# The 64-row operands of the last sequence chunk given 128 rows, and the last chunk of q 128 columns

## The chip, the cores and the metric

The kernel runs on one core of a Trainium2 chip. A core has five engines that work side by side and meet at semaphores: TensorE (PE in the rows; PEld is its loading of the stationary operand), VectorE (DVE), ScalarE (ACT), GpSimd (POOL) and SyncE (SP), which here only issues transfers. The metric is the device time of one execution in microseconds, lower is better.

## The reference, cut to what matters

Three blocks follow each other over a batch of 8 sequences of 576 tokens. All is float32.

```python
kv  = einsum('bhsd,bhse->bhde', k, v)          # attention without softmax: k^T v, 8 heads of 64
out = einsum('bhsd,bhde->bhse', q, kv)
x   = out / sqrt(mean(out*out, -1) + 1e-6) * g_norm

u   = x + ((x^T @ U) @ V)^T                    # token mixing of rank 32, over the 576 tokens
x   = u + relu(u @ w_ch1) @ w_ch2              # 512 -> 2048 -> 512

h   = gelu(x @ w_in)                           # 512 -> 1024; u, v are its halves
v_n = layernorm(v) * g_ln
v_s = einsum('ts,bsd->btd', w_sg, v_n) + b_sg  # token mixing by a 576 x 576 matrix
out = x + (u * v_s) @ w_out
```

## The kernel before

The 576 tokens of a sequence are cut into five chunks of rows: c = 0 to 3 have 128 tokens, c = 4 has 64 (`rows(c)`). The stationary operand of a matmul has up to 128 rows (what is summed over) and 128 columns (the partitions of the result). A matmul on float32 data (`F32` tiles) runs as two instructions, one on data split beforehand into a high and a low part (`F32R` tiles) as one, so that three products stand for one product of full precision. A transpose is one instruction.

The program on TensorE stands in the order in which the Python code issues it; the other engines' instructions are ordered by a scheduler at build time, by priority, and each engine then runs its own in that order. SyncE issues all transfers in order.

The part up to about 290 us of the span does the attention, the low-rank mixing and six of the sixteen column blocks of w_ch1. It goes batch by batch after the list `PERIOD`, one period of about 35 us each, in which the work of three batches is mixed: `U` is `ch1` of batch b (24 matmuls of 288 columns), and for the next batch b+1 come `X0` to `X4` (`att_x`, one chunk of q times kv, then on ScalarE a square and a copy out of PSUM, and on VectorE a sum), `T0` to `T4` (`att_t`, x^T U) and `D0` to `D3` (`att_u`, which transposes x by 128 columns, adds the mixing and writes `u` in a high and a low part), and for batch b+2 `K0` to `K3` (`att_kv`, k^T v of one pair of heads). `D` ends a period; `X0` to `X3` begin the next one, and the first `U` after them reads what `D` wrote. In the first period (b = 0, list `FIRST`) and the last (b = 7) `U` follows `D` at once. In front of the first period stands a start without other work to mix with.

- `att_kv`: for each chunk the k columns of one head (64 columns) are stationary and v streams; two heads' results lie in the lower and the upper 64 partitions of `kvps`. Chunks 0 to 3 come from `kvm` with 128 rows, chunk 4 from `kvr` with 64.
- `att_x`: a chunk of q is stationary (128 rows, `n` columns: 128, or 64 for chunk 4).
- `att_u`: `PARTS` are tokens 0 to 255 and 256 to 575. In each part the chunks are transposed (x chunk stationary, the identity streams) into one PSUM tile, and one matmul adds the mixing. Chunk 4 has 64 rows.
- `unit_s`, in the last part of the program (from about 950 us): the mixing by w_sg. The stationary operand is a chunk of v_n (`vh`, `vl`), w_sg streams in two halves of 288 columns. Chunks 0 to 3 take three products; in chunk 4 high and low part of v lie above each other in one tile of 128 rows, with w_sg's 64 rows twice, so that the first product covers both; the second takes the 64 rows of the high part alone (`v[r]`). `r` is the lower or the upper half in turn.

The PSUM ring `ar` of four buffers serves `kvps`, `xps` and `ups`; `uso`, a ring of three, serves the last part.

Of the kernel before, what the change touches and what calls it, by code (L numbers as in the profile page):

```python
# [12 lines left out]
F32 = mybir.dt.float32  # L13
# [3 lines left out]
AF = mybir.ActivationFunctionType  # L17
ALU = mybir.AluOpType
AX = mybir.AxisListType
# [3 lines left out]
B, H, S, D = 8, 8, 576, 64  # L23
# [3 lines left out]
P = 128  # L27
NP = H // 2
NC = 5
# [14 lines left out]
def rows(c):  # L44
    return P if c < 4 else S - 4 * P
# [14 lines left out]
def tile_kernel(ctx: ExitStack, tc: tile.TileContext, kvm, kvr, qt, gcol, uv, w12,  # L60
# [5 lines left out]
    nc = tc.nc  # L66
    mm = nc.tensor.matmul
# [78 lines left out]
    pm = ph0.enter_context(tc.tile_pool(name="pm", bufs=1, space=PSUM))  # L146
    at = ExitStack()
    ap = at.enter_context(tc.tile_pool(name="ap", bufs=1, side="right"))
# [8 lines left out]
    ident = ap.tile([P, P], F32, tag="ident", name="ident")  # L157
# [3 lines left out]
    kvbd = ap.tile([P, NP, P], F32, tag="kvbd", name="kvbd")  # L161

    kv_t, q_t = {}, {}

    def load_kv(b, p):
        if b < 2 and p >= 2:
            x = spare[2 + b][:, (p - 2) * 5 * 2 * P:(p - 1) * 5 * 2 * P].rearrange("p (c k) -> p c k", c=5)
            m, r = x[:, :4], x[:S - 4 * P, 4]
        else:
            m = ap.tile([P, 4, 2 * P], F32, tag="kvm", bufs=2, name="kvm")  # L170
            r = ap.tile([S - 4 * P, 2 * P], F32, tag="kvr", bufs=2, name="kvr")
        nc.sync.dma_start(m, kvm[b, p])
        nc.sync.dma_start(r, kvr[b, p])
        kv_t[b, p] = (m, r)

    def load_q(b, p):
        q = ap.tile([P, S], F32, tag=f"q{p}", name=f"q{p}")
        nc.sync.dma_start(q, qt[b, p])
        q_t[b, p] = q

    w_raw, wh, wl = {}, {}, {}
    raws_at = [12, 13, 6, 7]
# [61 lines left out]
    at_s = {}  # L244
# [18 lines left out]

    def att_x(b, c):

        n = rows(c)
        if c == 0:
            at_s["ss", b] = small(b, "ss", 0)
            nc.gpsimd.memset(at_s["ss", b][64:, 4], 1.0)
        ps = pm.tile([P, H, D], F32, tag="ar", bufs=4, name="xps")  # L270
        for p in range(NP):
            mm(ps[:n, 2 * p:2 * p + 2, :], q_t[b, p][:, c * P:c * P + n], kvbd[:, p, :],  # L272
               start=True, stop=True)
        xn = xn_of(b, c)
        if b or c % 2 == 0:
            sq = ap.tile([P, H, D], F32, tag="sq", name="sq")
        else:
            sq = spare[4][:, 2700:2700 + DM].rearrange("p (h d) -> p h d", h=H)
        nc.scalar.activation(sq[:n], ps[:n], AF.Square)
        nc.scalar.activation(xn[:n], ps[:n], AF.Copy)  # L280
        nc.vector.tensor_reduce(at_s["ss", b][:n, c], sq[:n], AX.X, ALU.add)
        at_s["x", b, c] = xn

    def att_root(b):
# [7 lines left out]
    def att_norm(b, cs):  # L292

        y = at_s["y", b]
        for c in cs:
            n = rows(c)
            xn = at_s["x", b, c]
            nc.vector.tensor_tensor(xn[:n], xn[:n], y[:n, c].unsqueeze(2).to_broadcast([n, H, D]),
                                    ALU.mult)
            xf = xn.rearrange("p h d -> p (h d)")  # L300
            xh = ap.tile([P, DM], F32R, tag="xh", bufs=2, name="xh")
            xl = xh[n:] if c == 4 else ap.tile([P, DM], F32R, tag="xl", bufs=2, name="xl")
            nc.scalar.activation(xh[:n], xf[:n], AF.Copy)
            nc.vector.tensor_sub(xl[:n], xf[:n], xh[:n].bitcast(F32))
            at_s["x", b, c] = xf, xh, xl
# [18 lines left out]
    def att_u(b, d):  # L324


        if d == 0:
            us[b] = [up.tile([P, ND, S], F32R, tag="u32", bufs=2, name=n) for n in ("uh", "ul")]
        t4 = at_s["t4", b]
        ds = slice(d * P, (d + 1) * P)  # L330
        u = mp.tile([P, S], F32, tag="ut", bufs=3, name="ut")
        for o, e, cs in PARTS:
            ps = pm.tile([P, S - 256], F32, tag="ar", bufs=4, name="ups")[:, :e - o]
            for c in cs:
                n = rows(c)
                xf = at_s["x", b, c][0]
                mm(ps[:, c * P - o:c * P - o + n], xf[:n, ds], ident[:n, :n], is_transpose=True,
                   start=(c == cs[0]), stop=False)
            mm(ps, t4[:, ds], v4[:, o:e], start=False, stop=True)
            if o:  # L340
                nc.vector.tensor_scalar_mul(u[:, o:e], ps, g)
            else:
                nc.scalar.activation(u[:, o:e], ps, AF.Identity, scale=g)
        nc.sync.dma_start(ud[b][:, d], u)
        uh, ul = us[b]
        nc.scalar.activation(uh[:, d], u, AF.Copy)  # L346
        nc.vector.tensor_sub(ul[:, d], u, uh[:, d].bitcast(F32))  # L347
# [133 lines left out]
    for p in range(NP):  # L481
        load_q(0, p)
    nc.gpsimd.memset(kvbd, 0.0)
    make_identity(nc, ident)
    tmp_u = next_tmp()[:, :nu]
    in_turn(convert(uvr[0][:, :nu], tmp_u))
# [46 lines left out]
    for b in range(B):  # L533
        n, n2 = (i if i < B else None for i in (b + 1, b + 2))
        i = 0
# [4 lines left out]
        for s in PERIOD if b else FIRST:  # L540
            c = int(s[1:] or 0)
# [42 lines left out]
    pm = pha.enter_context(tc.tile_pool(name="pmb", bufs=1, space=PSUM, reuse_waits="tile"))  # L584
# [112 lines left out]
    while units:  # L697
        n = 3 if len(units) == 3 else 2
        two, units = units[:n], units[n:]
        a, b = two[0], two[-1]  # L700
# [16 lines left out]
        if b.j == len(BLOCKS) - 1 and b.i in (0, 1):  # L717
            y = up.tile([P, ND, S], F32, tag="u32", bufs=2, name="y0")
# [227 lines left out]
    def unit_s(n, f):  # L946
        if f == 0:
            gh[n] = up.tile([P, ND, S], F32R, tag="u32", bufs=2, name="gh")
            gl[n] = up.tile([P, ND, S], F32R, tag="u32", bufs=2, name="gl")
        ps = uso()  # L950
        s = slice(f * P, (f + 1) * P)
        for c in range(NC):
            wgh, wgl = p2["wsgh"][:, c], p2["wsgl"][:, c]
            if c < 4:
                terms = ((vh[c], wgh), (vh[c], wgl), (vl[c], wgh))
            else:
                r = slice(64 * (n % 2), 64 * (n % 2) + 64)
                v = (vh, vl)[n % 2][c]
                terms = ((v, wgh), (v[r], wgl[r]))
            for i, (a, w) in enumerate(terms):  # L960
                for e in range(2):
                    mm(ps[:, e, :HS], a[:, s], w[:, halves[e]], start=(c == 0 and i == 0),  # L962
                       stop=(c == NC - 1 and i == 1))
        o = g2u.pop((n, f))
        t = pb.tile([P, S], F32, tag="ut", bufs=2, name="sq")
        nc.vector.scalar_tensor_tensor(halved(t), ps[:, :, :HS], gl2[:, f:f + 1], halved(bs2),
                                       ALU.mult, ALU.add)
        nc.vector.tensor_mul(t, t, o)
        nc.scalar.activation(gh[n][:, f], t, AF.Copy)
        lo = nc.vector if n == B - 1 else nc.gpsimd  # L970
        lo.tensor_sub(gl[n][:, f], t, gh[n][:, f].bitcast(F32))
# [41 lines left out]
    for n in range(B):  # L1013
        p = n - 1
# [8 lines left out]
        for s in seq:  # L1023
            i = int(s[1])
# [29 lines left out]
    n = B - 1  # L1054
# [56 lines left out]
```

## Time and profile before

| | before |
|---|---|
| median of 3 runs (lowest to highest) | 1377.82 us (1377.21 to 1380.42) |
| span of the profiled execution | 1374.1 us |
| TensorE busy in it | 1341.0 us, 98% |
| VectorE, ScalarE, GpSimd busy | 56%, 39%, 21% |
| TensorE's part of the chain that ended last | 88% |
| instructions of TensorE | 8050 matmuls, 8050 loads |

The span is counted from the first to the last recorded instruction of one execution. That execution's own device time isn't listed apart; the span lies 3.7 us below the median of the runs, which holds what stands before the first and behind the last instruction. A busy TensorE isn't a TensorE at its peak: a matmul's record is longer than the step from its start to the next one's start, because they overlap. So the text below works with starts.

### The profile page before, as it was taken

How to read it: one execution, taken by the hardware profiler on the slowest of the kernel's cores; microseconds unless marked ns; L12 is line 12 of the kernel's file. 1: busy time of each engine (PE TensorE's matmuls, PEld its weight loads, DVE VectorE, ACT ScalarE, POOL GpSimd, SP SyncE). 2: the span in 40 equal slices, each digit the busy share in tenths (PEclk: the TensorE clock that was granted, in tenths of full speed). 3: DMA queues.
4: the chain of work that ended last, by engine and by line, in shares of the span. 5: the costliest groups of instructions: out<-in, count | busy, mean ns of one | idle time of the engine just before them, and what ended most of it. 6: DMA issues, size and time to landing. Idle time of an engine off the chain costs nothing.

```text
span 1374.1 us, 20734 instructions
## 1 busy us (share of the span) xinstructions
PE 1341.0 (98%) x8050; PEld 1174.8 (85%) x8050; DVE 771.7 (56%) x1405; ACT 535.4 (39%) x888; POOL 284.7 (21%) x268
## 2 busy tenths in 40 slices
PE   6799999999999999999999999999999999999998
PEld 5599999997877789888888888889899999999998
DVE  4767777755765742322232234547676675775874
ACT  4665666654544532311211213445333333323321
POOL 0411001101111000200000001245253452543332
PEclk9999999999999999999999999999999999999999
DMA  9556665355766776835543545531021120110001
GB/s 347 191 190 221 218 214 182 107 180 185 271 221 220 245 261 244 318 93 170 167 144 114 171 161 192 168 108 44 1 70 36 35 70 18 52 53 18 36 18 52
DMA packets 86930, 199.44 MB, mean 145 GB/s; under 512 B 12208, under 2 KB 33456, under 8 KB 85040
## 3 DMA queue, kind: packets, MB, share of 16 engines
q1 hardware_dynamic: 86832, 198.12, 43.2%
q8 instruction: 63, 1.03, 0.3%
q14 instruction: 35, 0.29, 0.1%
HBM read 126.00 MB, written 72.09 MB: 144 GB/s over the span
## 4 chain that ended last, share of the span: by engine, by line
PE 88%; DVE 4%; ACT 1%; DMA 1%; issue 0%; POOL 0%; SPq 0%; DVEq 0%; ACTq 0%
PE acc L350 10%; PE acc L351 10%; PE acc L352 9%; PE uso L962 9%; PE uso L983 7%; PE uso L874 6%; PE c L350 4%; PE c L352 3%; PE c L351 3%; PE y L350 3%; PE y L352 3%; PE y L351 3%; PE v L350 2%; PE v L351 2%; PE v L352 2%; PE xps L272 2%
## 5 line engine op out<-in xcount | busy, mean ns | idle before, releaser
L350 PE MATMUL acc<-yx,w 128*128 128x512 f32 x576 | 224.1, 389 | 0.0
L352 PE MATMUL acc<-yx,w 128*128 128x512 f32 x576 | 224.1, 389 | 0.0
L351 PE MATMUL acc<-yx,w 128*128 128x512 f32 x576 | 224.1, 389 | 0.0
L772 DVE SCALAR_TENSOR_TENSOR yx<-yr,yx 128x1024 fp32r<-128x1024 f32 x70 | 85.8, 1226 | 244.1 <-ACT yx L771 237.1
L771 ACT ACTIVATE yx<-yr 128x1024 fp32r<-128x1024 f32 x70 | 74.3, 1061 | 277.4 <-PE acc L352 264.4
L350 PEld LDWEIGHTS acc<-yx,w 128*128 128x128 f32 x576 | 108.1, 188 | 22.6 <-ACT y L604 0.2
L352 PEld LDWEIGHTS acc<-yx,w 128*128 128x128 f32 x576 | 108.1, 188 | 22.5
L351 PEld LDWEIGHTS acc<-yx,w 128*128 128x128 f32 x576 | 108.1, 188 | 22.2
L350 PE MATMUL c<-uh,w 128*128 128x288 f32 x384 | 116.7, 304 | 0.7 <-ACT uh L346 0.7
L351 PE MATMUL c<-ul,w 128*128 128x288 f32 x384 | 113.6, 296 | 1.8 <-DVE ul L347 1.8
L352 PE MATMUL c<-uh,w 128*128 128x288 f32 x384 | 113.4, 295 | 0.8 <-POOL w L126 0.6
L874 PE MATMUL uso<-zh,wio 128*128 128x288 f32 x512 | 94.2, 298 | 0.6 <-DVE g2u L882 0.4
L983 PE MATMUL uso<-gh,wio 128*128 128x288 f32 x512 | 93.1, 296 | 0.0
L109 POOL TENSOR_TENSOR tmp<-tmp,wior 128x512 int32<-128x512 int32 x12 | 15.7, 1309 | 314.7 <-DVE tmp L108 269.8
L983 PEld LDWEIGHTS uso<-gh,wio 128*128 128x128 f32 x512 | 77.9, 188 | 2.3 <-issue 0.2
L350 PE MATMUL y<-T,c 128*128 128x512 f32 (+1 forms) x200 | 75.3, 376 | 4.1 <-DVE y L602 3.7
L874 PEld LDWEIGHTS uso<-zh,wio 128*128 128x128 f32 x512 | 76.3, 188 | 3.2 <-issue 1.3
L350 PEld LDWEIGHTS c<-uh,w 128*128 128x128 f32 x384 | 72.0, 188 | 4.1 <-issue 1.0
L351 PEld LDWEIGHTS c<-ul,w 128*128 128x128 f32 x384 | 72.1, 188 | 3.8 <-DVE ul L347 2.9
L351 PE MATMUL y<-T,c 128*128 128x512 f32 (+1 forms) x200 | 74.5, 372 | 0.0
L352 PE MATMUL y<-T,c 128*128 128x512 f32 (+1 forms) x200 | 74.5, 372 | 0.0
L352 PEld LDWEIGHTS c<-uh,w 128*128 128x128 f32 x384 | 72.1, 188 | 1.3 <-POOL w L126 0.9
(210 smaller groups left out, 2916.4 us busy)
## 6 DMA issues: line engine op xcount, KB each, us to landing
yr<-yd SPq DMA_DIRECT2D x70, 512.0 KB, 3.7
yd<-y SPq DMA_DIRECT2D x92, 256.0 KB, 3.4
kvm<-kvm_dram SPq DMA_DIRECT2D x28, 512.0 KB, 4.6
raw<-w_dram SPq DMA_DIRECT2D x26, 512.0 KB, 4.2
q<-qt_dram SPq DMA_DIRECT2D x32, 288.0 KB, 4.8
ud<-ut SPq DMA_DIRECT2D x32, 288.0 KB, 2.1
z<-ud SPq DMA_DIRECT2D x8, 1152.0 KB, 6.4
out_dram<-ot SPq DMA_DIRECT2D x31, 288.0 KB, 2.1
```

What stands on the lines that cost most here:

```text
L109: yield behind(nc.gpsimd.tensor_add(t, t, low))
L272: mm(ps[:n, 2 * p:2 * p + 2, :], q_t[b, p][:, c * P:c * P + n], kvbd[:, p, :], start=True, stop=True)
L350: mm(ps, ah, bh, start=start, stop=False, **kw)
L351: mm(ps, ah, bl, start=False, stop=False, **kw)
L352: mm(ps, al, bh, start=False, stop=stop, **kw)
L771: nc.scalar.activation(yh, y, AF.Relu)
L772: nc.vector.scalar_tensor_tensor(yl, y, 0.0, yh.bitcast(F32), ALU.max, ALU.subtract)
L874: mm(ps[:, e, :HS], a[:, s], c[:, halves[e]], start=(d == 0 and i == 0), stop=(d == ND - 1 and i == 2))
L962: mm(ps[:, e, :HS], a[:, s], w[:, halves[e]], start=(c == 0 and i == 0), stop=(c == NC - 1 and i == 1))
L983: mm(ops[d][:, e, :HS], a[:, s], c[:, f, halves[e]], start=(f == 0 and i == 0), stop=(f == ND - 1 and i == 2))
```

## The change

Each operand of 64 rows becomes one of 128 rows, with zeros or with a second copy in the added rows.

- `kvr` and the spare tiles that hold its data in the first two batches have 128 rows; the lower half is set to zero by GpSimd (two tiles at the start for all batches, one memset for each of the four spare slices). The transfers write the upper half, as before.
- q lives in four fixed tiles `q_of` of 640 columns; the last 64 are set to zero once, in four memsets. Chunk 4 of `att_x` takes 128 columns, so that its results have 128 rows, the lower 64 of them zero. The eight memsets on `ss` that kept the unused rows harmless are gone.
- `att_u` transposes chunk 4 with 128 rows and 128 columns; the PSUM tile has 384 columns instead of 320, of which 320 are used.
- `unit_s` takes the whole `v` and `wgl` in the second product of chunk 4: the low part times the low part is added to the sum.

```diff
@@ -162,21 +162,28 @@
 
     kv_t, q_t = {}, {}
 
+    rest = [ap.tile([P, 2 * P], F32, tag=f"kvr{i}", name="kvr") for i in range(2)]
+    q_of = [ap.tile([P, NC * P], F32, tag=f"q{p}", name=f"q{p}") for p in range(NP)]
+    for r in rest:
+        nc.gpsimd.memset(r[rows(4):], 0.0)
     def load_kv(b, p):
         if b < 2 and p >= 2:
             x = spare[2 + b][:, (p - 2) * 5 * 2 * P:(p - 1) * 5 * 2 * P].rearrange("p (c k) -> p c k", c=5)
-            m, r = x[:, :4], x[:S - 4 * P, 4]
+            m, r = x[:, :4], x[:, 4]
+            nc.gpsimd.memset(r[rows(4):], 0.0)
         else:
             m = ap.tile([P, 4, 2 * P], F32, tag="kvm", bufs=2, name="kvm")
-            r = ap.tile([S - 4 * P, 2 * P], F32, tag="kvr", bufs=2, name="kvr")
+            r = rest[p % 2]
         nc.sync.dma_start(m, kvm[b, p])
-        nc.sync.dma_start(r, kvr[b, p])
+        nc.sync.dma_start(r[:rows(4)], kvr[b, p])
         kv_t[b, p] = (m, r)
 
     def load_q(b, p):
-        q = ap.tile([P, S], F32, tag=f"q{p}", name=f"q{p}")
-        nc.sync.dma_start(q, qt[b, p])
-        q_t[b, p] = q
+        nc.sync.dma_start(q_of[p][:, :S], qt[b, p])
+        q_t[b, p] = q_of[p]
 
     w_raw, wh, wl = {}, {}, {}
     raws_at = [12, 13, 6, 7]
@@ -263,22 +270,20 @@
 
     def att_x(b, c):
 
-        n = rows(c)
         if c == 0:
             at_s["ss", b] = small(b, "ss", 0)
-            nc.gpsimd.memset(at_s["ss", b][64:, 4], 1.0)
         ps = pm.tile([P, H, D], F32, tag="ar", bufs=4, name="xps")
         for p in range(NP):
-            mm(ps[:n, 2 * p:2 * p + 2, :], q_t[b, p][:, c * P:c * P + n], kvbd[:, p, :],
+            mm(ps[:, 2 * p:2 * p + 2, :], q_t[b, p][:, c * P:(c + 1) * P], kvbd[:, p, :],
                start=True, stop=True)
         xn = xn_of(b, c)
         if b or c % 2 == 0:
             sq = ap.tile([P, H, D], F32, tag="sq", name="sq")
         else:
             sq = spare[4][:, 2700:2700 + DM].rearrange("p (h d) -> p h d", h=H)
-        nc.scalar.activation(sq[:n], ps[:n], AF.Square)
-        nc.scalar.activation(xn[:n], ps[:n], AF.Copy)
-        nc.vector.tensor_reduce(at_s["ss", b][:n, c], sq[:n], AX.X, ALU.add)
+        nc.scalar.activation(sq, ps, AF.Square)
+        nc.scalar.activation(xn, ps, AF.Copy)
+        nc.vector.tensor_reduce(at_s["ss", b][:, c], sq, AX.X, ALU.add)
         at_s["x", b, c] = xn
 
     def att_root(b):
@@ -295,8 +300,7 @@
         for c in cs:
             n = rows(c)
             xn = at_s["x", b, c]
-            nc.vector.tensor_tensor(xn[:n], xn[:n], y[:n, c].unsqueeze(2).to_broadcast([n, H, D]),
-                                    ALU.mult)
+            nc.vector.tensor_tensor(xn, xn, y[:, c].unsqueeze(2).to_broadcast([P, H, D]), ALU.mult)
             xf = xn.rearrange("p h d -> p (h d)")
             xh = ap.tile([P, DM], F32R, tag="xh", bufs=2, name="xh")
             xl = xh[n:] if c == 4 else ap.tile([P, DM], F32R, tag="xl", bufs=2, name="xl")
@@ -330,11 +334,11 @@
         ds = slice(d * P, (d + 1) * P)
         u = mp.tile([P, S], F32, tag="ut", bufs=3, name="ut")
         for o, e, cs in PARTS:
-            ps = pm.tile([P, S - 256], F32, tag="ar", bufs=4, name="ups")[:, :e - o]
+            full = pm.tile([P, NC * P - 256], F32, tag="ar", bufs=4, name="ups")
+            ps = full[:, :e - o]
             for c in cs:
-                n = rows(c)
                 xf = at_s["x", b, c][0]
-                mm(ps[:, c * P - o:c * P - o + n], xf[:n, ds], ident[:n, :n], is_transpose=True,
+                mm(full[:, c * P - o:(c + 1) * P - o], xf[:, ds], ident, is_transpose=True,
                    start=(c == cs[0]), stop=False)
             mm(ps, t4[:, ds], v4[:, o:e], start=False, stop=True)
             if o:
@@ -481,6 +485,8 @@
     for p in range(NP):
         load_q(0, p)
     nc.gpsimd.memset(kvbd, 0.0)
+    for q in q_of:
+        nc.gpsimd.memset(q[:, S:], 0.0)
     make_identity(nc, ident)
     tmp_u = next_tmp()[:, :nu]
     in_turn(convert(uvr[0][:, :nu], tmp_u))
@@ -954,9 +960,8 @@
             if c < 4:
                 terms = ((vh[c], wgh), (vh[c], wgl), (vl[c], wgh))
             else:
-                r = slice(64 * (n % 2), 64 * (n % 2) + 64)
                 v = (vh, vl)[n % 2][c]
-                terms = ((v, wgh), (v[r], wgl[r]))
+                terms = ((v, wgh), (v, wgl))
             for i, (a, w) in enumerate(terms):
                 for e in range(2):
                     mm(ps[:, e, :HS], a[:, s], w[:, halves[e]], start=(c == 0 and i == 0),
```

The order on TensorE is the same but for the shapes. The next rows are TensorE's, in `D0` to `D1` of batch 1 (end of the first period), of before and then of the change; `ups` is the PSUM tile, `xn` the normalized chunk, `t` the mixing's operand, and the sizes are those of what is written.

```order
L337 MATMUL ups<-ident,xn 128x128 x2
L339 MATMUL ups<-v_119,t_836 128x256
L337 MATMUL ups<-ident,xn 128x128 x2
L337 MATMUL ups<-ident,xn 128x64
L339 MATMUL ups<-v_119,t_836 128x320
L337 MATMUL ups<-ident,xn 128x128 x2
```

```order
L341 MATMUL ups<-ident,xn 128x128 x2
L343 MATMUL ups<-v_119,t_828 128x256
L341 MATMUL ups<-ident,xn 128x128 x3
L343 MATMUL ups<-v_119,t_828 128x320
L341 MATMUL ups<-ident,xn 128x128 x2
```

The transpose of chunk 4 writes 128 columns instead of 64; nothing stands at another place.

GpSimd's first work after its constants, before and then with the change; `kvbd` is the block-diagonal kv, `ident` the identity.

```order
L483 MEMSET kvbd 128x512
masks.py:197 MEMSET ident 128x128
L269 MEMSET spare_127 64x8
L269 MEMSET ss 64x8
masks.py:199 ISA
masks.py:199 AFFINE_SELECT ident<-ident 128x128
L109 TENSOR_TENSOR tmp_121<-tmp_121,uv_140 128x160
```

```order
L170 MEMSET kvr 64x256 x2
L176 MEMSET spare_133 64x256 x2
L487 MEMSET kvbd 128x512
L489 MEMSET q_123 128x64
L489 MEMSET q_124 128x64
L489 MEMSET q_125 128x64
L489 MEMSET q_126 128x64
masks.py:197 MEMSET ident 128x128
L176 MEMSET spare_134 64x256
masks.py:199 ISA
masks.py:199 AFFINE_SELECT ident<-ident 128x128
L176 MEMSET spare_134 64x256
```

Ten memsets of zeros stand among the first, two small ones are gone, and `kvbd` comes fifth.

VectorE's work around the first `D0` to `D3` (batch 0, end of the start), before and then with the change; `ny` and `nt` are the reciprocal root of batch 1, `ut` and `ul` belong to `D`, `xn` and `xl` to the chunks of batch 1.

```order
L341 TENSOR_SCALAR ut<-ups,g 128x320
L94 SCALAR_TENSOR_TENSOR ny<-nt,ny 128x40
L92 TENSOR_TENSOR nt<-ny 128x40
L93 SCALAR_TENSOR_TENSOR nt<-nt,ss 128x40
L94 SCALAR_TENSOR_TENSOR ny<-nt,ny 128x40
L347 TENSOR_TENSOR ul<-ut,uh 128x576
L341 TENSOR_SCALAR ut<-ups,g 128x320 x2
L298 TENSOR_TENSOR xn<-xn,ny 128x512
L347 TENSOR_TENSOR ul<-ut,uh 128x576 x2
L341 TENSOR_SCALAR ut<-ups,g 128x320
L304 TENSOR_TENSOR xl<-xn,xh 128x512
L298 TENSOR_TENSOR xn<-xn,ny 128x512
```

```order
L345 TENSOR_SCALAR ut<-ups,g 128x320
L92 TENSOR_TENSOR nt<-ny 128x40
L93 SCALAR_TENSOR_TENSOR nt<-nt,ss 128x40
L94 SCALAR_TENSOR_TENSOR ny<-nt,ny 128x40
L303 TENSOR_TENSOR xn<-xn,ny 128x512
L351 TENSOR_TENSOR ul<-ut,uh 128x576
L345 TENSOR_SCALAR ut<-ups,g 128x320 x2
L308 TENSOR_TENSOR xl<-xn,xh 128x512
L351 TENSOR_TENSOR ul<-ut,uh 128x576 x2
L345 TENSOR_SCALAR ut<-ups,g 128x320
L303 TENSOR_TENSOR xn<-xn,ny 128x512 x2
L351 TENSOR_TENSOR ul<-ut,uh 128x576
```

One scaling of a chunk (`xn`) more stands ahead of the fourth `ul`, and the first `ut` one small instruction later. From the second period on VectorE's order differs in sizes alone but for one exchange in the first period, and ScalarE's by an exchange of neighbours in `X0` and `X1`.

## Rows read from the trace of the kernel before

**Rows 1.** The page, first part: busy time, share of the span, instructions.

```profile
PE 1341.0 (98%) x8050; PEld 1174.8 (85%) x8050; DVE 771.7 (56%) x1405; ACT 535.4 (39%) x888; POOL 284.7 (21%) x268
```

**Rows 2.** Busy time by stretch; behind the engines: granted clock, share of DMA, GB/s.

```profile
114.71:123.17 8.46, 8.18 (x63) 7.05 (x61) 5.48 (x9) 6.54 (x13) 0.00 (x0) 1.00 0.58 212
540.00:920.00 380.00, 380.00 (x1678) 314.77 (x1677) 126.95 (x167) 98.15 (x112) 33.09 (x26) 1.00 0.52 173
950.00:1365.00 415.00, 413.41 (x2721) 384.77 (x2720) 282.66 (x605) 136.43 (x217) 166.15 (x159) 1.00 0.11 35
```

**Rows 3.** Whom TensorE waited for: us in total, times, longest.

```profile
PE ups L339 <- DVE nt L92: 7.3, 1, 7.3
...
PE c L351 <- DVE ul L347: 1.8, 4, 0.7
PE tp L315 <- DVE xl L304: 1.4, 2, 1.1
```

**Rows 4.** Timeline of TensorE, chunk 4 of one unit_s (start, length, rows*columns, count).

```profile
1304.43 0.43 PE L962 MATMUL uso<-wsgh,vh 128*128 128x288 f32 x2
1304.79 0.52 PE L962 MATMUL uso<-wsgl,vh 64*128 64x288 f32 x2
1305.24 0.53 PE L962 MATMUL uso<-wsgh,vh 128*128 128x288 f32 x2
1305.61 0.42 PE L962 MATMUL uso<-wsgl,vh 128*128 128x288 f32 x2
1305.87 0.43 PE L962 MATMUL uso<-wsgh,vl 128*128 128x288 f32 x2
```

**Rows 5.** Timeline of TensorE, end of one att_kv, from narrow windows (last instructions of each).

```profile
112.53 0.29 PE L255 MATMUL kvps<-kvm 128*64 128x64 f32 x4
...
112.59 0.23 PE L255 MATMUL kvps<-kvm 128*64 128x64 f32 x2
112.75 0.27 PE L255 MATMUL kvps<-kvr 64*64 64x64 f32 x2
...
112.85 0.23 PE L255 MATMUL kvps<-kvr 64*64 64x64 f32 x2
113.01 0.40 PE L350 MATMUL c<-uh,w 128*128 128x288 f32 x1
```

**Rows 6.** Timeline of TensorE, D0 of batch 2 and the start of D1.

```profile
114.71 0.38 PE L337 MATMUL ups<-ident,xn 128*128 128x128 f32 x2
...
115.05 0.58 PE L337 MATMUL ups<-ident,xn 128*128 128x128 f32 x3
...
115.81 0.38 PE L337 MATMUL ups<-ident,xn 128*128 128x128 f32 x2
```

**Rows 7.** Timeline of TensorE, X0 and X1 (two windows), then X4 of batch 3.

```profile
119.13 1.05 PE L272 MATMUL xps<-kvbd,q 128*128 128x128 f32 x8
...
119.13 1.95 PE L272 MATMUL xps<-kvbd,q 128*128 128x128 f32 x16
...
124.70 0.29 PE L352 MATMUL c<-uh,w 128*128 128x288 f32 x1
124.92 1.09 PE L272 MATMUL xps<-kvbd,q 128*64 128x128 f32 x8
...
126.18 0.30 PE L351 MATMUL c<-ul,w 128*128 128x288 f32 x1
```

**Rows 8.** Timeline of ScalarE, the square of X0 of batch 3; in brackets the idle time before.

```profile
120.22 0.60 ACT L279 ACTIVATE sq<-xps 128x512 f32<-128x512 f32 x1 [0.65 <-PE xps L272]
```

**Rows 9.** Timeline of TensorE, waits in the first and in the last period.

```profile
66.94 0.40 PE L352 MATMUL c<-uh,w 128*128 128x288 f32 x1 [0.63 <-POOL w L126]
...
293.59 0.40 PE L351 MATMUL c<-ul,w 128*128 128x288 f32 x1 [0.23 <-DVE ul L347]
```

**Rows 10.** Timeline of the start: the first memset, and the first chunk of 64 rows.

```profile
0.74 0.53 POOL L483 MEMSET kvbd<- 128x512 f32 x1 [0.29 <-POOLq L1096]
...
5.30 0.37 PE L255 MATMUL kvps<-kvr 64*64 64x64 f32 x2
```

## The prediction

> **What bounds the kernel now.** First the page's list of busy engines: TensorE is busy for 98% of the span [rows 1]. That alone doesn't say that it sets the pace everywhere, so the busy time by stretch comes next: from 540 to 920 us it has no gap, in the last part (950 to 1365 us) 1.6 us of 415, and around a `D` to `X` passage (114.71 to 123.17 us) 0.3 us of 8.5 [rows 2]. The list of waits agrees: single waits at the start and around `D` and `T`, nearly none later [rows 3]. So a step that TensorE saves comes off the span, unless the next thing it needs isn't ready. What it could save is read from the starts in its timeline, since the records overlap.
>
> **What an operand of 64 rows costs.** In `unit_s`, with 128 rows, two matmuls of 288 columns take 0.26 us from start to start (1305.61 to 1305.87) [rows 4]. Around chunk 4 the pairs start at 1304.43, 1304.79, 1305.24 and 1305.61: 1.18 us for three pairs, where 3 x 0.26 = 0.78 would do [rows 4]. The 0.40 us aren't work, since the 64-row pair streams the same 288 columns. They come half on the way into 64 rows and half on the way out, and TensorE names no releaser for them. I read them as the price of going from one array shape to another and back, about 0.2 us each way. By the Trainium skill (TensorEngine Tiling (Array Packing), Key Properties) a change of tiling mode drains TensorE; the rows agree, and as it gives no figure the sum is made from the rows.
>
> **The change, part by part.**
>
> `unit_s`: 32 visits (8 batches of 4 units), each with its two shape changes gone and nothing added, since the second product streams 288 columns either way: 32 x 0.39 = 12.5 us (0.39 and not 0.40, as the starts have two decimals). The stretch has 1.6 us of waits in all and VectorE is busy for 283 of 415 us, so I take all of it as span [rows 2].
>
> `att_u`: a `D` takes 115.81 - 114.71 = 1.10 us; its first part, two transposes of 128 and a matmul of 256 columns, takes 0.34 [rows 6]. The second part will be three transposes and 320 columns without a change of shape; scaled by streamed columns, 0.34 x 704 / 512 = 0.47. So a `D` takes 0.81 and saves 0.29, four save 1.16. What is late next? ScalarE and VectorE empty the PSUM tiles. In the `D` to `X` passage ScalarE is busy 6.54 us of 8.46 [rows 2], and in front of the square of `X0` it sat idle for 0.65 us until TensorE had finished `X0` [rows 8]. With a passage of 7.3 us it still fits, with little left; I count 1.1 instead of 1.16 in the six periods where `X` follows `D` (batches 1 to 6): 6.6 us. After the `D` of batch 7 the next `U` waits for VectorE's `ul` already [rows 9]; there I count 0.4 of 1.16, since the first `ut` comes earlier by only a part. The `D` of batch 0 lies in the start, see below: 0.
>
> `att_x`, chunk 4: from the last matmul before it (124.70) to the second after it (126.18) 1.48 us [rows 7]. With 128 columns throughout: eight instructions take 1.95 - 1.05 = 0.90 us (`X1` alone), plus 0.13 for each of the two `U` matmuls that belong to the stretch: 1.16, so 0.31 saved [rows 4, 7]. The added columns of the load cost next to nothing: the 64-column chunk has a record of 1.09 us, `X0` with 128 columns one of 1.05 [rows 7]. In five of the eight batches it lies in a period whose next wait is far enough away: 5 x 0.31 = 1.6 us. In batch 7's `T` TensorE waits for VectorE's `xl`, whose chain starts at the squares [rows 3]: there the 0.31 are lost and about 0.3 us more of the saved time turns into waiting, -0.3.
>
> By the Trainium skill (TensorE: Matmul & The Clock Gate, LDWEIGHTS) a load's time goes with its columns, not its rows: 64 more columns would add an estimated 53 ns to each of 64 loads, 3.4 us, were they not hidden. The rows speak against that, as the loads lie beside matmuls. For the added rows the same rule says no cost, as I assume.
>
> `att_kv`: pairs of 128-row instructions start 0.06 apart (112.53, 112.59), the pair of `kvr` comes after 0.16, the next after 0.10, and the `U` matmul 0.16 later: 0.42 from the last `kvm` pair [rows 5]. With 128 rows the operand has the shape of `kvm`: 0.06 + 0.06 + 0.16 = 0.28. The change of shape at the end stays, since 64 columns remain. 0.14 saved; 24 visits in the periods, of which the first two stand ahead of a wait in the first period (below): 22 x 0.14 = 3.1 us.
>
> The start and the first period: ten memsets of 64 rows come first on GpSimd. `kvbd` with 512 columns took 0.53 us [rows 10]; at that rate the four ahead of it take 4 x 0.27 = 1.1 us, and all ten no more than 2.6. The first matmul of 64 rows starts at 5.30 us [rows 10], so they lie under the first transfers; no transfer waits for them in SyncE's order. Uncovered they'd cost up to 2.6 us once. Later the start hangs on VectorE: TensorE waits 7.3 us in it [rows 3], so the 64-row visits before that are worth nothing there, but for an estimated 0.3 us (the last `kvr` of batch 0 and its `X4`, some 0.15 each) ahead of VectorE's first work. The new order puts one more scaling of 512 columns ahead of the fourth `ul` of batch 0; a square of 512 columns takes ScalarE 0.60 [rows 8], and about 0.6 I take for this. TensorE then waits at 66.94 for weights that GpSimd and VectorE split behind it [rows 9]. So nothing from ahead of 67 us comes through, and 0.3 us net are lost.
>
> **The sum.** 12.5 + 6.6 + 0.4 + 1.6 - 0.3 + 3.1 - 0.3 = 23.6 us. The span goes from 1374.1 to 1350.5. The median of the runs shown lies 3.7 us above the span; I take the same distance: 1377.8 - 23.6 = 1354.2 us.
>
> **Rivals.**
>
> *All of it arrives*: every visit at its full price, 32 x 0.39 + 32 x 0.29 + 8 x 0.31 + 32 x 0.14 = 12.5 + 9.3 + 2.5 + 4.5 = 28.8 us, 1349.0. For it: the six passages show little waiting. Against: waits stand behind the first and the last `D` [rows 3, 9].
>
> *The first part swallows its share*: ScalarE and VectorE set the pace of `D`, `X` and `T`, and of 11 us there half or all is waited for again. That gives 1360 to 1365. For it: 6.54 us of ScalarE's work in a passage that shrinks to 7.3 [rows 2]. Against: its 0.65 us of idle time, which would have to vanish first [rows 8].
>
> *The change of rows isn't what costs*: the 0.4 us come from chunk 4's operands themselves (the upper half of a tile, a stop of the group), and remain. Then only the start's 0.3 us and some 0.01 us an `X4` are added: 1378. Against: `att_kv`, `att_u` and `att_x` show delays of like size in other operands with nothing in common but the shape [rows 5 to 7].
>
> *Slower, through the clock*: a fuller array makes TensorE's granted clock fall in the last part. A stretch of t us that falls from the upper level (2.4 GHz) to the lower (1.2) takes t longer; to eat the 23.6 us, 23.6 of the 415 us would have to run at the lower one (a mean grant of 0.94), and at 0.90 the time would be 1396. Against: from 540 to 920 us all operands have 128 rows and no gap, and the grant is 1.00 [rows 2].
>
> **How the numbers follow.** Forecast 0.68 (19 to 27 us, 1351 to 1359), all of it 0.12, swallowed 0.14, no effect 0.04, slower 0.02. A difference of 0.3% (4.1 us) is about what a measurement of this kernel can tell from none. The first three are faster: 0.94; same 0.04; slower 0.02. The predicted time is 1354.2. The range takes in the forecast, the full price and the nearer third of the swallowed case: 1349 to 1361; left out are some 0.15.
>
> **What would show it.** In the changed profile: pairs of `unit_s` at 0.26 us throughout, no record with 64 rows on TensorE, 64 columns left in `att_kv` alone; the stretch between the first and the last `unit_s` shorter by some 12 us; a `D` of 0.81 us; each period of the first part shorter by 4 x 0.29 + 0.31 + 4 x 0.14 = 2.0 us. Wrong would be: gaps of 0.2 us that remain around chunk 4; waits of TensorE for `xn` or `ul` of 1 us in each period; a grant below 1.00 behind 950 us.

## The result and the profile after

| | before | after |
|---|---|---|
| median, 4 runs each (lowest to highest) | 1378.59 us (1377.21 to 1380.42) | 1354.05 us (1352.97 to 1354.84) |
| ratio, 95% interval | | 0.9824 [0.9812, 0.9836] |
| span of the profiled execution | 1374.1 us | 1352.0 us |

The time fell by 24.5 us; 23.6 were forecast, and the predicted 1354.2 us lies 0.15 us from the measured median.

The first line of the page, which answers to [rows 1], shows that TensorE is still busy nearly throughout. Its part of the chain that ended last is 83% of the span (88% before), VectorE's 8% (4% before). Its busy time fell by 26.1 us, 4.0 more than the span. VectorE, ScalarE and GpSimd have what they had, to 2 us.

```profile
PE 1314.9 (97%) x8050; PEld 1170.9 (87%) x8050; DVE 773.5 (57%) x1405; ACT 533.4 (39%) x888; POOL 286.0 (21%) x270
```

The next rows answer to [rows 2]: busy time by stretch of the kernel after, columns as there. Both stretches begin and end with the same instructions of TensorE as before, to within one matmul.

```profile
112.64:119.94 7.30, 7.02 (x62) 6.83 (x61) 5.56 (x10) 6.25 (x13) 0.00 (x0) 1.00 0.71 261
938.81:1343.02 404.21, 401.79 (x2721) 383.09 (x2720) 282.61 (x605) 135.99 (x217) 166.00 (x159) 1.00 0.11 36
```

The `D` to `X` passage is 1.16 us shorter (8.46 to 7.30), four times 0.29. The last part is 10.8 us shorter (415.00 to 404.21), and in it TensorE idles 2.4 us where it idled 1.6. The granted clock is 1.00 in both: a fuller array hasn't lowered it.

The list of TensorE's waits after (us in total, times, longest) answers to [rows 3].

```profile
PE ups L343 <- DVE nt L92: 7.5, 1, 7.5
...
PE c L355 <- DVE ul L351: 2.5, 5, 0.7
...
PE tp L319 <- DVE xl L308: 1.7, 2, 1.1
PE uso L880 <- DVE g2u L888: 1.4, 3, 0.6
PE uso L967 <- DVE g2u L888: 0.9, 1, 0.9
PE acc L355 <- DVE yx L778: 0.8, 1, 0.8
```

The big wait of the start is the same. Those for `ul` (1.8 before), `xl` (1.4) and for VectorE's `g2u` in the last part (0.4 and 0.9) have grown by 0.7, 0.3 and 1.0 us. So VectorE takes back about 2 us in all: it was on time for the old pace and is a little late for the new one. The wait for `yx` is a new row, of which more below.

The visits themselves, from TensorE's timeline after: chunk 4 of a `unit_s` for [rows 4], then the same view of an `att_kv` for [rows 5], `D0` of batch 2 for [rows 6] and an `X4` for [rows 7].

```profile
1284.99 0.43 PE L967 MATMUL uso<-wsgh,vh 128*128 128x288 f32 x2
1285.26 0.42 PE L967 MATMUL uso<-wsgl,vh 128*128 128x288 f32 x2
1285.52 0.43 PE L967 MATMUL uso<-wsgh,vh 128*128 128x288 f32 x2
1285.79 0.42 PE L967 MATMUL uso<-wsgl,vh 128*128 128x288 f32 x2
```

```profile
109.97 0.30 PE L356 MATMUL c<-uh,w 128*128 128x288 f32 x1
110.20 0.69 PE L262 MATMUL kvps<-kvm 128*64 128x64 f32 x16
110.71 0.29 PE L262 MATMUL kvps<-kvr 128*64 128x64 f32 x4
110.93 0.40 PE L354 MATMUL c<-uh,w 128*128 128x288 f32 x1
111.17 0.30 PE L355 MATMUL c<-ul,w 128*128 128x288 f32 x1
...
112.64 0.38 PE L341 MATMUL ups<-ident,xn 128*128 128x128 f32 x2
112.77 0.37 PE L343 MATMUL ups<-v,t 128*128 128x256 f32 x1
112.98 0.49 PE L341 MATMUL ups<-ident,xn 128*128 128x128 f32 x3
113.22 0.40 PE L343 MATMUL ups<-v,t 128*128 128x320 f32 x1
113.45 0.38 PE L341 MATMUL ups<-ident,xn 128*128 128x128 f32 x2
...
121.47 0.30 PE L356 MATMUL c<-uh,w 128*128 128x288 f32 x1
121.61 1.05 PE L277 MATMUL xps<-kvbd,q 128*128 128x128 f32 x8
122.42 0.38 PE L354 MATMUL c<-uh,w 128*128 128x288 f32 x1
122.63 0.29 PE L355 MATMUL c<-ul,w 128*128 128x288 f32 x1
```

In `unit_s` the pairs start 0.26 to 0.27 us apart throughout, where the steps around chunk 4 were 0.36, 0.45 and 0.37 [rows 4]. A `D` takes 113.45 - 112.64 = 0.81 us. Around `X4` it is 122.63 - 121.47 = 1.16. No operand has 64 rows any more; 64 columns remain in `att_kv` alone, and there 0.22 us still pass from the start of the `kvr` record (four instructions) to the next `U` matmul.

ScalarE's square of `X0` of batch 3 after, for [rows 8]:

```profile
117.00 0.60 ACT L284 ACTIVATE sq<-xps 128x512 f32<-128x512 f32 x1
```

The 0.65 us for which it sat idle ahead of this square are gone: ScalarE now comes from work of `D` straight to it. Its reserve in the passage is used up, but it isn't late: the square starts 1.09 us behind the first matmul of its `X0`, as before (119.13 to 120.22, [rows 7, 8], and 115.91 to 117.00).

### The profile page after: what moved, and what is told of

Read it like the earlier page. It is cut to its first block, busy times and chain, and to the rows that moved or that the text cites. A ratio compares the mean times of both kernels' runs of the same rounds, so it can differ in the third digit from the quotient of the medians.

```text
span 1352.0 us, 20734 instructions
## 1 busy us (share of the span) xinstructions
PE 1314.9 (97%) x8050; PEld 1170.9 (87%) x8050; DVE 773.5 (57%) x1405; ACT 533.4 (39%) x888; POOL 286.0 (21%) x270
## 3 DMA queue, kind: packets, MB, share of 16 engines
q8 instruction: 63, 1.03, 0.3%
## 4 chain that ended last, share of the span: by engine, by line
PE 83%; DVE 8%; DMA 4%; ACT 3%; issue 2%; POOL 0%; SPq 0%; DVEq 0%; ACTq 0%; POOLq 0%
PE acc L355 9%; PE acc L356 9%; PE acc L354 9%; PE uso L967 8%; PE uso L988 6%; PE uso L880 5%; PE c L354 4%; PE c L355 4%; PE c L356 3%; PE y L354 3%; PE y L355 3%; PE y L356 3%; PE v L355 2%; PE v L354 2%; PE v L356 2%
```

## The experiments

All ratios are to the kernel before, in runs on the same chip. First the change is taken apart. Each of the four parts alone:

**The part in `unit_s` alone** (the kernel before with the last hunk of the diff):

```diff
-                terms = ((v, wgh), (v[r], wgl[r]))
+                terms = ((v, wgh), (v, wgl))
```

> The kernel before with the change of unit_s alone. Shape theory (each going from one array shape to another costs TensorE about 0.1 to 0.2 us, whatever the operand holds): 32 visits of 0.39 us less, minus the waits of about 1.2 us for VectorE that the changed kernel shows in this part, so 11 us less than before, about 1367. Rival that the last part is set by VectorE and only gets its time back from the earlier parts: under 4 us less, above 1374.

Measured: 1367.23 us, 0.9921 [0.9906, 0.9936], 11.0 us less. Its waits in the last part:

```profile
PE uso L961 <- DVE g2u L882: 1.0, 1, 1.0
PE uso L874 <- DVE g2u L882: 0.9, 2, 0.5
```

Before they were 0.9 and 0.4. The saved time is what the visits give, less a little that is waited for behind them.

**All but `unit_s`** (the kernel after with that hunk undone):

> The change without its part in unit_s (att_kv, att_x and att_u alone). Shape theory: 24 x 0.14 + 6 x 0.32 + 28 x 0.29 = 13.4 us of visits, minus about 2 us that come back as waits at the start, at the first U of the last period and behind it: 11 to 12 us less than before, about 1367. Rival that ScalarE and VectorE set the pace in the first part: half of it or less, above 1372.

Measured: 1365.92 us, 0.9907 [0.9893, 0.9922], 12.3 us less. The two halves add up to 23.3, the whole is 24.5: the halves don't help or hinder each other beyond what the runs scatter.

**The part in `att_u` alone.** Chunk 4 of x has zeros in the added rows because `att_x` makes them; alone it needs a memset for each batch, on GpSimd, whose cost is part of this run.

```diff
+        if c == 4:
+            nc.gpsimd.memset(xn[n:], 0.0)
...
-                mm(ps[:, c * P - o:c * P - o + n], xf[:n, ds], ident[:n, :n], is_transpose=True,
+                mm(full[:, c * P - o:(c + 1) * P - o], xf[:, ds], ident, is_transpose=True,
```

> The kernel before with the change of att_u alone (the added rows of the chunk are set to zero by GpSimd in each batch). Shape theory: 28 D at 0.29 us, 8.1, of which about 0.8 comes back at the first U of the last period and up to 1 us in the X that follow: 6 to 7.5 us less than before, about 1371. Rival that ScalarE and VectorE set the pace from D to X: 3 us less or none, 1375 or above, with TensorE waiting 0.5 us or more for xn or ut in each period.

Measured: 1370.21 us, 0.994 [0.9925, 0.9955], 8.6 us less. The added transposed columns, which nobody reads, cost less than the two changes of shape that they avoid.

**The part in `att_kv` alone** (`kvr` with 128 rows, the lower ones zeros):

```diff
-            r = ap.tile([S - 4 * P, 2 * P], F32, tag="kvr", bufs=2, name="kvr")
+            r = rest[p % 2]
...
```

> The kernel before with the change of att_kv alone (the transfers and the zeroed rows of kvr). Shape theory: 24 visits at 0.14 us, the first two without effect: 3 us less, about 1375.5; in the trace 0.58 to 0.60 us from the first kvm matmul to the last pair instead of 0.72. Rival that the second pair's delay is the load's, not the shape's: less than 1.5 us.

Measured: 1375.60 us, 0.9981 [0.9971, 0.9990], 3.0 us less.

**The part in `att_x` alone** (q in tiles of 640 columns, 128 columns in chunk 4):

```diff
-            mm(ps[:n, 2 * p:2 * p + 2, :], q_t[b, p][:, c * P:c * P + n], kvbd[:, p, :],
+            mm(ps[:, 2 * p:2 * p + 2, :], q_t[b, p][:, c * P:(c + 1) * P], kvbd[:, p, :],
...
```

> The kernel before with the change of att_x alone (q of 640 columns, chunk 4 with 128 columns). Shape theory: six visits at 0.32 us, of which the one of batch 7 may come back as a wait in T: 1.6 to 1.9 us less, about 1376.7, close to what these runs can tell from nothing; in the trace 1.16 us from the matmul before X4 to the second behind it instead of 1.48. Rival that the load's added columns count: 8 x 0.05 = 0.4 us of it lost per X4, no gain.

Measured: 1376.99 us, 0.9988 [0.9979, 0.9997], 1.6 us less; its interval and that of the part before it just leave 1 out. The four parts give 11.0 + 8.6 + 3.0 + 1.6 = 24.2 of the 24.5 us.

Next, is it the shape that costs, or the operands of chunk 4 themselves? That was the rival by which nothing would happen.

**Two visits in place of one.** In the kernel before, the two 64-row matmuls of each `unit_s` are put around the 128-row pair. The work is the same; only the order changes, so that TensorE goes to 64 rows twice.

```diff
+            if c == NC - 1:
+                pairs = [(1, 0), (0, 0), (0, 1), (1, 1)]
+            for i, e in pairs:
...
```

> The kernel before, in which the two matmuls of 64 rows of each unit_s no longer stand together: one comes ahead of the pair with 128 rows and one behind it. The same matmuls with the same operands, but two visits to the 64-row shape per unit instead of one. Shape theory: 32 more visits at 0.39 us, 12.5 us slower than before, about 1391. Rival (the cost lies in the 64-row operands themselves, in their half of the tile or their load): same time as before, 1378. Rival (the cost lies at the end of a unit's sum): same or up to 6 us less.

Measured: 1389.74 us, 1.0083 [1.0068, 1.0098], 11.5 us more. TensorE's timeline around chunk 4 in this kernel:

```profile
1307.96 0.43 PE L965 MATMUL uso<-wsgh,vl 128*128 128x288 f32 x2
1308.32 0.39 PE L965 MATMUL uso<-wsgl,vh 64*128 64x288 f32 x1
1308.64 0.53 PE L965 MATMUL uso<-wsgh,vh 128*128 128x288 f32 x2
1309.11 0.40 PE L965 MATMUL uso<-wsgl,vh 64*128 64x288 f32 x1
1309.44 0.40 PE L874 MATMUL uso<-zh,wio 128*128 128x288 f32 x1
```

Each single 64-row matmul now takes 0.32 or 0.33 us to the next start, where 0.13 would do, and the 128-row pair between them 0.47 instead of 0.26. A second visit costs 11.5 / 32 = 0.36 us, about as much as the first.

**The same order with 128 rows** (the kernel after with those lines). It tells the change of shape from the change of order.

> The changed kernel with the order of the run that visited the 64-row shape twice per unit_s: the second product's two matmuls stand around the first product's, all with 128 rows now. Shape theory: nothing changes shape, so the time of the changed kernel, 1354 within 0.1%. Rival that the order of the matmuls (which half of PSUM they add to, where the sum of a half ends) made that run slow: 1366.

Measured: 1354.47 us, 0.9826 [0.9811, 0.9840], the time of the kernel after. With equal shapes the order is worth nothing, with unequal shapes 11.5 us. With these two runs I call it shown that a change of the operand's shape is what costs, some 0.2 us for each change between these matmuls.

How it costs can be read from the loads. The next rows are TensorE's loads in the kernel before, at the chunk 4 of [rows 4]:

```profile
1304.43 0.19 PEld L962 LDWEIGHTS uso<-wsgh,vh 128*128 128x128 f32 x1
1304.79 0.29 PEld L962 LDWEIGHTS uso<-wsgl,vh 64*128 64x128 f32 x2 [0.17 <-issue]
1305.24 0.19 PEld L962 LDWEIGHTS uso<-wsgh,vh 128*128 128x128 f32 x1 [0.16 <-issue]
```

The load of 1304.43 belongs to the second matmul of the pair that starts then, at 1304.56: it lies 0.13 us ahead of it, beside the first one. The first load of 64 rows, at 1304.79, and the first of 128 rows after it, at 1305.24, start together with their own matmuls instead [rows 4]. So at a change of shape the next load doesn't run ahead, and nothing that the profile shows holds it back ("issue"). Why it doesn't is not shown. The Trainium skill (TensorEngine Tiling (Array Packing), Key Properties) says that changing the tiling mode drains TensorE. The rows agree, if the operand's shape is taken for that mode, which no row names.

The visits to 64 columns in `att_kv` are left. Two ways to be rid of them were tried on the kernel after.

**Full columns.** Both heads' k are stationary at once and both v stream: one instruction of 128 columns and 128 results in place of two of 64. The off-diagonal blocks of the result mix two heads and aren't read.

```diff
-                for j in range(2):
-                    mm(acc[j * D:(j + 1) * D, p, :], src[:, j * D:(j + 1) * D],
-                       src[:, P + j * D:P + (j + 1) * D], start=(c == 0), stop=(c == NC - 1))
+                mm(acc[:, p, :], src[:, :P], src[:, P:], start=(c == 0), stop=(c == NC - 1))
```

> The changed kernel with the last change of shape taken out of att_kv too: the k columns of both heads are stationary together (128 columns) and both heads' v stream (128 columns), one matmul instead of two per chunk; the two blocks off the diagonal are computed and not used. Shape theory: the switches saved are paid for with streaming. A visit takes 0.23 + 0.73 + 0.24 = 1.19 us in the changed kernel from the matmul before it to the second behind it; with 10 instructions at 0.111 us it is 0.13 + 1.11 + 0.13 = 1.38. So 0.19 us more, 22 to 24 times: 4 us slower than the changed kernel, about 1358. Rival that every change of shape is worth taking out: 24 x 0.34 = 8 us less, about 1346.

Measured: 1358.46 us, 0.9856 [0.9839, 0.9872], 4.4 us slower than the kernel after. TensorE's timeline over one such `att_kv`:

```profile
93.28 0.29 PE L354 MATMUL c<-uh,w 128*128 128x288 f32 x1
93.41 1.05 PE L261 MATMUL kvps<-kvm 128*128 128x128 f32 x8
94.30 0.39 PE L261 MATMUL kvps<-kvr 128*128 128x128 f32 x2
94.44 0.38 PE L352 MATMUL c<-uh,w 128*128 128x288 f32 x1
94.66 0.29 PE L353 MATMUL c<-ul,w 128*128 128x288 f32 x1
```

From the `U` matmul ahead to the second behind it 1.38 us pass. In the kernel after it is 1.20 (109.97 to 111.17 in the rows for [rows 5] above). The changes of shape are gone, but the ten instructions of 128 columns take longer than the twenty of 64: 1.03 us to the next `U` matmul against 0.73 with both changes of shape. So padding isn't free: it pays where few instructions stand in a visit.

**Fewer visits.** `K0 K1` and `K2 K3` side by side, so that two `att_kv` share one visit; the list `FIRST` is changed in the same way.

```diff
-    PERIOD = "X0 X1 X2 X3 U X4 U U K0 U K1 U T0 T1 U U T2 T3 U U T4 U K2 U K3 U D0 D1 D2 D3".split()
+    PERIOD = "X0 X1 X2 X3 U X4 U U K0 K1 U U T0 T1 U U T2 T3 U U T4 U K2 K3 U U D0 D1 D2 D3".split()
```

> The changed kernel with K0 and K1 of a period side by side, and K2 and K3, instead of a U between them: the 64-column shape that the change leaves in att_kv is entered and left 12 times instead of 24. Shape theory: each visit saved is worth 0.09 + 0.05 + 0.10 + 0.10 = 0.34 us (entry, second pair, exit, second matmul behind it), 4 us less than the changed kernel, about 1350. Rival (only rows matter, not columns): the time of the changed kernel, 1354. Rival (T or K wait for transfers or for xl, now that a U stands elsewhere): 1354 or above, with waits of TensorE for kvm or xl.

Measured: 1353.28 us, 0.9814 [0.9798, 0.9830]; the expected 4 us below the kernel after didn't come. The four runs lie far apart (1351.01 to 1355.90 us), and the profiled one is the slowest of them. The shared visit is there, in TensorE's timeline: from the `U` matmul ahead to the second one behind 1.77 us pass for two. Two single visits take 2 x 1.20, less the 0.26 of two `U` matmuls that stand in both, which is 2.14. So a shared visit saves 0.37, about the 0.34 that was expected, and a visit to 64 columns has its price too.

```profile
93.32 0.29 PE L356 MATMUL c<-uh,w 128*128 128x288 f32 x1
93.54 0.69 PE L262 MATMUL kvps<-kvm 128*64 128x64 f32 x16
...
94.86 0.40 PE L354 MATMUL c<-uh,w 128*128 128x288 f32 x1
95.09 0.29 PE L355 MATMUL c<-ul,w 128*128 128x288 f32 x1
```

In this execution what it saves goes into new waits. In the list of waits from 75 to 305 us, ScalarE and VectorE now wait for the transfer that stores `u` before they can write the next `ut`, and TensorE's `X` waits for them:

```profile
ACT ut L347 <- DMA ud<-ut: 4.2, 5, 1.6
DVE ut L345 <- DMA ud<-ut: 3.3, 4, 1.4
...
PE xps L277 <- ACT ut L347: 2.1, 2, 1.9
```

In the same list of the kernel after, the first row has 0.6, the second is missing, and the third has 0.6.

At the first `U` of batch 7 the wait for `ul` has become 1.57 us long, and TensorE's clock fell behind it. The busy time by stretch of the same kernel, columns as in [rows 2]:

```profile
280.00:283.50 3.50, 1.69 (x10) 1.22 (x11) 1.98 (x3) 1.16 (x2) 0.00 (x0) 1.00 0.60 199
283.50:287.00 3.50, 3.50 (x18) 3.50 (x17) 0.00 (x0) 1.16 (x3) 0.00 (x0) 0.51 0.92 286
```

TensorE was busy for 1.69 us of the 3.50 in the first row, and in the next 3.5 the grant is 0.51, the lower level (1.2 GHz): 14 matmuls start 0.24 apart instead of 0.13, which costs 1.5 us.

**A fourth buffer for `ut`** says whether the store is to blame. It takes its room from the ring of `y`, which goes from three buffers to two; in the kernel after, and then with the visits shared:

```diff
-        u = mp.tile([P, S], F32, tag="ut", bufs=3, name="ut")
+        u = mp.tile([P, S], F32, tag="ut", bufs=4, name="ut")
-            yt[b] = mp.tile([P, S], F32, tag="y", bufs=3, name="y")
+            yt[b] = mp.tile([P, S], F32, tag="y", bufs=2, name="y")
```

> The changed kernel with four tiles for u in att_u instead of three (and two instead of three for y in ch1, to have the space). Theory of the new wait (with shorter D the fourth D of a batch waits until the first one's u has been stored, and ScalarE and VectorE wait with it): the 0.6 us of such waits in the changed kernel go, and up to 1 us at the first U of the last period: 0.5 to 1.5 us less, about 1353. Rival that this wait is covered anyway: no difference. Rival that two y tiles are too few: 1 us or more slower, with ScalarE waiting for the store of y.

Measured: 1352.28 us, 0.9809 [0.9795, 0.9824], 1.8 us below the kernel after; the intervals overlap.

> The changed kernel with K0 and K1, K2 and K3 side by side and with four tiles for u. Theory: the run with the K side by side lost its 4 us to waits for the store of u (ScalarE 4.2 and VectorE 3.3 us, against 0.6 and 0 in the changed kernel) and to 3.3 us at the lower clock that followed one of them. With the fourth tile both go: 1349 to 1350. Rival that moving the K costs by itself (U and T wait elsewhere): 1353 as before.

Measured: 1350.92 us, 0.9799 [0.9784, 0.9813], the fastest version here, 3.1 us below the kernel after and 27.9 below the kernel before. No wait of the first part names the store of `u` any more (the smaller ring costs 0.9 us of TensorE's time, in a wait for ScalarE's `y`). The first of the next rows is from the list of TensorE's waits from 75 to 305 us, the second covers the stretch in which the clock had fallen:

```profile
PE tp L319 <- DVE xl L308: 2.0, 6, 0.6
...
283.50:287.00 3.50, 3.50 (x29) 3.50 (x28) 2.45 (x2) 0.95 (x4) 0.00 (x0) 1.00 1.06 362
```

With the fourth buffer the waits behind the store and the fall of the clock are gone, so in the profiled execution the store held the shared visits back. The medians point the same way, but each of the steps from one of these four kernels to the next is about as large as their intervals. The rival isn't out either: TensorE's waits for `xl` in `T` have grown from 0.6 us in the kernel after to 2.0, so moving the `K` costs something by itself. Matched start by start, the stretch of 80 to 276 us is 1.7 us shorter than in the kernel after, where ten shared visits would give 3.5. What made the store late in that order (the transfers queued ahead of it, or the moved `U`) was not tried.

## Why the prediction was right, point by point

The starts of TensorE's instructions, matched one by one between the two profiled executions, say where the span's 22.1 us came from. Their sums by stretch, worked out from the traces:

| stretch of the kernel before | predicted | measured |
|---|---|---|
| start, up to 80 us, with two visits of `att_kv` | +0.3 - 0.3 = 0.0 | +0.4 |
| 80 to 276 us, the periods, with `T` of batch 7 | -6.6 - 1.6 - 2.8 + 0.3 = -10.7 | -11.8 |
| 276 to 305 us, `D` of batch 7 and behind | -0.4 | -0.4 |
| 305 to 950 us | 0 | +0.6 |
| from 950 us | -12.5 | -10.9 |
| sum | -23.6 | -22.1 |

**What a 64-row operand costs.** Right, and the main reason for the result: prices of 0.39 (`unit_s`), 0.29 (`D`), 0.31 (`X4`) and 0.14 us (`att_kv`) were read from [rows 4 to 7] before anything ran, and the starts after give 0.39, 0.29, 0.32 and 0.14. The two runs with the split order show the cause in `unit_s`; in the other three places it rests on the parts run alone and on the same delays going away. By the rule of the Trainium skill on load times (TensorE: Matmul & The Clock Gate, LDWEIGHTS) the wider loads of `att_x` would have cost an estimated 3.4 us, were they not hidden. No run shows that cost: the part of `att_x` alone is 1.6 us faster than before, and its record of eight instructions is 1.05 us long where it was 1.09 [rows 7].

**`unit_s`: 12.5 us.** The price was right, the cover wrong by 1.6 us. I took all 32 visits as span because TensorE waited 1.6 us in 415. It waits 0.8 us more now (2.4 in the matched stretch), nearly all for `g2u`, with which VectorE frees a buffer of the `uso` ring. Start by start, 29 of the visits give 0.39 us each, 11.2 in all; the other three have such a wait right behind them, and there 0.3 us are lost where 1.2 were counted as saved. A mean VectorE load of 282 in 404 us says nothing about the three places where its chain was just in time.

**`att_u`, `att_x`, `att_kv`: 11.0 us in the periods.** Right to 1.1 us: 10.7 of the 11.0 lie behind 80 us, and 11.8 came. A period is 1.8 to 2.5 us shorter where 2.0 were forecast; the shortest gain has a wait of 0.56 us in it, for a `ut` of ScalarE. The reserve of ScalarE in front of `X0` was the step on which it rested: it was 0.65 us, and it is now 0 [rows 8], yet no wait of 1 us per period followed. The rival by which half of this is waited for again fails on that. Alone, the parts gave 8.6, 1.6 and 3.0 us, where their terms are 7.0, 1.3 and 3.1; the first is larger by less than its interval.

**Batch 7.** From its `X4` to the end of its first `T` TensorE gains nothing (0.1 us lost, worked out from the starts): the 0.3 of `X4` goes into the wait for `xl`, as forecast, and 0.1 more with it instead of the 0.3 that the sum had. Then the `D` saves 1.16 us, and 0.4 of it remains, as forecast, since the first `U` behind it waits for `ul`: TensorE's timeline after, with the idle time in brackets, for [rows 9].

```profile
280.86 0.40 PE L355 MATMUL c<-ul,w 128*128 128x288 f32 x1 [0.65 <-DVE ul L351]
281.77 0.40 PE L355 MATMUL c<-ul,w 128*128 128x288 f32 x1 [0.24 <-DVE ul L351]
```

**The start: 0.3 us lost.** At 67 us TensorE was 0.7 us later than before, but neither the memsets nor VectorE's new order can be blamed for it: with `unit_s` changed alone, and with its two visits, where the start is word for word that of before, TensorE is at 80 us 0.7 and 1.4 us later than before. Here executions of one program differ by more than the term. They differ in TensorE's clock too: its mean grant over the first 80 us is 0.94 in the profile of before and 0.89 in those two and in that of after. How much of the delay comes from it isn't shown. The memsets are done within 4 us on GpSimd, ahead of the first matmul of 64 former rows, as [rows 10] let expect. From GpSimd's timeline after, the last of them:

```profile
3.66 0.31 POOL L176 MEMSET spare<- 64x256 f32 x1
```

**What I hadn't counted.** Between 305 and 950 us the sum says 0, and 0.6 us were lost. At one place, the first `acc` of a later stage, where VectorE's `yx` is late, it was 1.1, and 0.5 came back at a wait for `y` that was shorter:

```profile
538.74 0.50 PE L355 MATMUL acc<-yx,w 128*128 128x512 f32 x1 [0.76 <-DVE yx L778]
```

This is scatter between executions and not the change's doing: `unit_s` changed alone and `unit_s` with two visits, which are the kernel before up to there, wait 0.4 and 0.6 us for the same `yx`, and the change without `unit_s`, which is the kernel after up to there, has no wait at this place.

I also read the waits of before too lightly. Between 300 and 540 us they come to 4.6 us, 3.7 of them for VectorE's `y`, where I wrote nearly none [rows 3]. No operand of 64 rows stands there, so the sum doesn't hang on it.

**From span to median.** The median fell by 24.5, the span by 22.1. In the runs of after whose span is listed the device time lies 2.0 us above it; I had taken 3.7, from the median of before over one span. The profiled execution of before was therefore one of its faster ones, by about 2 us. TensorE's clock goes with this: the mean grant over that execution is 0.996, and among the 33 further runs of before whose span is listed the two with 0.996 have 1375.5 and 1375.6 us, the nine with 0.992 have 1376.9 on the mean. That close a hit on 1354.2 is partly luck: a forecast of 1350.5 for the span met 1352.0.

## What to carry to other kernels

Read steps from start to start, and look for matmuls of another operand shape amid full ones: here a lone visit to 64 rows cost 0.29 to 0.39 us beside its work, and zeros or a second copy in the free rows removed it at no cost that these runs can tell from scatter. Padding has its limit, which the same rows tell: `att_kv` with full columns, ten instructions of 128 columns instead of twenty of 64, lost more than the two changes of shape cost. There fewer, longer visits, with a buffer more behind them, were the better way, though the runs tell that step only just. When TensorE gains time, look next at the engine that was just in time at single places, not at its mean load, and at the ring whose buffers a store has to free.

## What the hardware showed unexpectedly

A wait of 1.57 us, with little work around it (TensorE busy for 1.69 of 3.50 us), was followed by TensorE's clock at its lower level and a further 1.5 us lost, in a stretch that was otherwise dense. With `att_u` changed alone the same came once more: a wait of 1.76 us at 318.64 us (TensorE busy for 1.74 of 3.50 us), and then a grant of 0.50. The length of the wait doesn't decide it: the kernel with the shared visits also waits 1.69 us for `y` at 315.88 us, and 1.89 us at 186.14 (the row below), and neither is followed by a fall.

```profile
186.14 0.38 PE L277 MATMUL xps<-kvbd,q 128*128 128x128 f32 x1 [1.89 <-ACT ut L347]
```

In the kernel after, with waits of 0.42, 0.65 and 0.24 us at the same place, the grant stayed at 1.00. The Trainium skill (TensorE: Matmul & The Clock Gate, Part 1) says that the clock follows how busy TensorE has lately been. Both falls agree with that; what sets them apart from the waits without a fall was not tried.
